# Pooled attention and an affine ResMLP on one core: loads moved to ScalarE's queue, and q's last rows transposed directly behind the fourth chunk of u

## Chip, cores and metric

The kernel runs on one NeuronCore of a Trainium2 chip. The metric is device time in microseconds: the median of seven runs is 348.65 us (345.37 to 350.87). The engines are named as in the profile: PE is TensorE, DVE VectorE, ACT ScalarE, POOL GpSimd, SP SyncE. SP computes nothing here, it issues DMAs; ACT and POOL can issue DMAs too. PEld is the loading of weights into PE.

## The reference: what is computed

Eight batches of attention with 8 heads, 576 rows and a head width of 64, whose keys and values are first averaged over groups of 8 rows (72 groups). Its result, with the heads side by side as 512 columns, goes through token mixing over the 576 rows and a two-layer network with 2048 hidden columns:

```
k_p = k.reshape(B, H, Sp, pool, D).mean(axis=3)        # pool = 8, Sp = 72
v_p = v.reshape(B, H, Sp, pool, D).mean(axis=3)
scores = scale * np.matmul(q, k_p.transpose(0, 1, 3, 2))
attn = softmax(scores);  x = attn @ v_p                # heads side by side: (B, 576, 512)
a1 = alpha1 * x + beta1
u = x + lam * np.einsum('ts,bsd->btd', w_tok, a1)
ch = np.maximum((alpha2 * u + beta2) @ w_ch1, 0.0) @ w_ch2
out = u + lam * ch
```

Inputs and output are float32; matrix products run in 16-bit types.

## The kernel before

**Chunks and blocks.** The output rows are cut into chunks of 128: four for each batch (rows 0 to 511), and one that holds the last 64 rows of two neighbouring batches (c = 4, made in the odd batch). The 36 chunks are lined up and taken four at a time, so there are nine blocks n = 0 to 8. A block runs the network on four chunks: `mlp_A(n, j)` (L640) makes hidden tile j of 16 (four matmuls into ps_h at L651, a relu to Hj on ACT at L657), and `mlp_B(n, m, part)` (L662) makes the output of chunk m in four parts of four matmuls (ps_ch, L686). After part 3, DVE adds the result to u (L692, L693) and SP stores it (L695, L699).

**Attention of the next batch inside the block.** Block n also works on batch b = n + 1, through `attention(b)` (L789): sums of v (DVE, L479) and of k (POOL, `sum_k`, L183 and L185), pooled keys (`att_K`), scores (`att_S4`, L500, which reads qT for the first 512 rows at L511 and rem_qT for the last 64 at L518), exponentials on ACT, the product with v (`att_AV`), x_tm on DVE (L563) and xs = x times lam and alpha1 (`att_X`, L577). Then `mix_T(b, c)` (L602) does token mixing: five matmuls into ps_tok that read xs (L609), then u_sb (L613) and u_bf (L616) on DVE. `mix_uT` (L618) transposes u_bf into u_fm, the input of a later block: from block 1 on as a crossbar (transposing) DMA on SP (L625). The chunks made in block n are used in block n + 1 in part: block 1 needs all four chunks of batch 1, block 2 the first three of batch 2 and the shared chunk before them, block 3 again the first three of batch 3, later blocks fewer of the newest batch.

**Loads.** In block n the inputs of batch b + 1 = n + 2 are loaded: q for rows 0 to 511 by POOL with a cast to bf16 (`load_q_bf`, L79), k by `load_k` (L88, two DMAs of 512 KB), v by `load_v` (L153), and the last 64 rows of q and k by `load_rem` (L141, four DMAs of 64 KB). Up to now k, v and the last rows go out on SP, except at the start. POOL's `cast_rem` (L164) turns the last rows into rem_q and rem_k; `att_Frem` (L410) transposes rem_q into rem_qT by a crossbar DMA on SP (L415) from b = 2 on; `att_F` (L382) does it for q's main part (L391).

**What sets the order.** The tile pools have a manual schedule: each piece of work carries a number, its place in the block, and L875 sorts the list and emits it. The sort is stable, and the items of mlp_A and mlp_B are put into the list first (L841 to L850), so at equal numbers they come first. mlp_A(j) has place j, mlp_B in blocks from 1 on 16 + 4m + part. In block 0 the first two chunks alternate:

```
        for m in range(4):
            for part in range(4):
                at = 16 + (2 * part + m if n == 0 and m < 2 else 4 * m + part)
                todo.append((at, lambda m=m, part=part: mlp_B(n, m, part)))
```

Each engine and each issuing queue then goes through its own instructions in that order. `first` in `attention` is b == 1, that is block 0. The places beside the change: mlp_B in block 0 at 16 to 31; the store of a chunk comes with its part 3; `mix_uT` has the place of its mix_T plus 1.8; `cast_rem(b + 1)` is at 24.5 (25.6 in block 0), `sum_k(b + 1)` at -0.9 and 0.3 of the next block, directly followed on POOL by that block's q loads at 0.4 and 0.5. On ACT the last work of a block from 1 on is at 15.35 (the last exponentials), the next is the first Hj of the next block.

Of the kernel before, what the change touches and what calls it, by code (L numbers as in the profile page):

```python
# [23 lines left out]
def kernel(  # L24
# [18 lines left out]
    nc = tc.nc  # L43
# [8 lines left out]
    def gp(name):  # L52
        return psA.tile([P, 512], FP, tag="gp", name=name)
# [17 lines left out]
    def rows(src, b, u):  # L71
        return src[b, 4 * u:4 * u + 4, 0:512, :].rearrange("h (p c) d -> p h (c d)", c=4)
# [15 lines left out]
    def load_k(b, u, behind=None, queue=nc.sync):  # L88

        raw = work.tile([P, 4, 4, D], FP, tag="k_raw", bufs=2, name="k_raw")  # L90
        if behind is not None:
            behind.memset(raw[:, 0, 0, 0:1], 0.0)
        queue.dma_start(out=raw.rearrange("p h c d -> p h (c d)"), in_=rows(k, b, u))
        st1[b]["raw"][u] = raw
# [46 lines left out]
    def load_rem(b, queue=nc.sync, behind=None):  # L141

        raw = work.tile([P, 2, 2, 2, D], FP, tag="rem_raw", bufs=2, name="rem_raw")
        if behind is not None:
            behind.memset(raw[:, :, :, 0, 0:1], 0.0)
        for i, src in enumerate((q, k)):
            for h in range(2):
                (nc.scalar if h and not b else queue).dma_start(
                    out=raw[:, i, h].rearrange("p c d -> p (c d)"),
                    in_=src[b, h::2, 512:576, :].rearrange("a (i c) d -> i a (c d)", c=2))  # L150
        st1[b]["rem_raw"] = raw
# [12 lines left out]
    def cast_rem(b, eng, copy=None):  # L164
        raw = st1[b]["rem_raw"]
        rq = work.tile([P, 2, 2, D], BF, tag="rem_q", bufs=2, name="rem_q")
        rk = work.tile([P, 2, 2 if b else 3, D], BF, tag="rem_k", bufs=2, name="rem_k")
        (copy or eng.tensor_copy)(out=rq.rearrange("p c h d -> p h c d"), in_=raw[:, 0])
        twice = [raw[:, 1, :, c].unsqueeze(2).to_broadcast((P, 2, 2, D)) for c in range(2)]
        if b:  # L170
            eng.tensor_tensor(out=rk, in0=twice[0], in1=twice[1], op=ALU.add)
        st1[b]["rem"] = rq, rk
# [190 lines left out]
    def load_w2(g):  # L363
        nc.gpsimd.dma_start(
            out=w2[g], in_=moe_w_ch2[512 * g:512 * g + 512, :].rearrange("(p i) d -> p i d", i=4))

    def scale_w2(g):
        nc.vector.tensor_tensor(
            out=w2[g], in0=w2[g], in1=lam_bc.unsqueeze(1).to_broadcast((P, 4, DM)), op=ALU.mult)
# [40 lines left out]
    def att_Frem(b, copy=None):  # L410

        st = st1[b]
        st["rem_qT"] = work.tile([P, 2, P], BF, tag="rem_qT", bufs=2, name="rem_qT")
        if copy is None:
            nc.sync.dma_start_transpose(out=st["rem_qT"],  # L415
                                        in_=st["rem"][0].rearrange("p c h d -> p (c h d)"))
            return
        ps_q = gp("ps_qr").bitcast(BF)
        for c in range(2):
            nc.tensor.transpose(out=ps_q[:, 128 * c:128 * c + 128],  # L420
                                in_=st["rem"][0][:, c].rearrange("p h d -> p (h d)"),
                                identity=identity_bf)
        copy(out=st["rem_qT"], in_=ps_q[:, 0:256].rearrange("p (c t) -> p c t", c=2))
# [365 lines left out]
    def attention(b):  # L789


        first = b == 1
        todo = []
        if first:
            for hp in range(4):
                todo.append((2.6 + 0.9 * hp, lambda hp=hp: att_F(b, hp)))
            todo.append((3.5, lambda: cast_rem(b, nc.gpsimd)))
            for u in range(2):
                todo.append((3.65 + 0.1 * u, lambda u=u: load_w2(2 + u)))
            todo.append((7.4, lambda: att_Frem(b, nc.scalar.copy)))  # L800
        if b < B - 1:
            at = 28.5 if first else 10.0
            todo.append((at, lambda: att_F(b + 1, 0)))
            todo.append((at + 0.1, lambda: att_F(b + 1, 2)))
            todo.append((25.6 if first else 24.5, lambda: cast_rem(b + 1, nc.gpsimd)))
            todo.append((27.5, lambda: att_Frem(b + 1)))
        for u in range(2):
            todo.append((3.6 + 0.1 * u if first else -0.9 + 1.2 * u,
                         lambda u=u: sum_k(b, u, nc.gpsimd)))
            todo.append((7.0 + 2.3 * u if first else 4.1 + 2.0 * u,  # L810
                         lambda u=u: att_K(b, u, nc.vector.tensor_copy)))
        for u in range(2):
            at = (9.0 if first else 6.3, 13.6)[u]
            todo.append((at, lambda u=u: att_S4(b, u)))
            for k, dt in enumerate((0.1, 0.1, 0.1, 0.7, 1.7, 1.75) if u else (0.1, 0.1, 0.1, 1.1, 2.1, 3.1)):
                todo.append((at + dt, lambda u=u, k=k: st1[b]["exp", u](k)))
            early = (5.7, 6.2, 4.2, 4.7) if first else (5.7, 6.2, 2.9, 3.4)
            for i, dt in enumerate((2.9, 3.4, 4.6, 5.1) if u else early):
                h = 4 * u + i
                todo.append((at + dt, lambda h=h: att_AV(b, h)))  # L820
                if i % 2:
                    eng = nc.gpsimd if h == 5 or first and h < 5 else nc.vector
                    todo.append((at + dt + 0.1, lambda h=h, eng=eng: att_X(b, h - 1, h + 1, eng)))
        if first:
            for i, u in enumerate((0, 2, 1)):
                todo.append((10.6 + 0.1 * i, lambda u=u: sum_v(b, u)))
            for u in range(2):
                todo.append((12.3 + 1.0 * u, lambda u=u: first_V(b, u)))
        for hp in range(0 if first else 4):
            todo.append((0.2 + 2.0 * hp, lambda hp=hp: att_V(b, hp)))  # L830
        for c in range(5):
            at = 21.0 + 1.3 * c
            if c < 4 or b % 2:
                todo.append((at, lambda c=c: mix_T(b, c)))
                key = (b, c) if c < 4 else (b - 1, 4)
                todo.append((at + 1.8, lambda key=key: mix_uT(key)))
        return todo

    for n in range(NBLK):
        todo = []  # L840
        for j in range(0 if n else 4, NJ):  # L841
            if n == 0 and j < 8:
                todo.append((j, lambda j=j: mlp_A(0, j, 0, 256)))
                todo.append((j + (1.01 if j < 7 else 0.3), lambda j=j: mlp_A(0, j, 256, 512)))
            else:
                todo.append((j, lambda j=j: mlp_A(n, j)))
# [4 lines that stand above are left out]
        if n == 0:  # L851
            todo.append((6.2, lambda: setup_rowsum(4)))
            todo.append((8.3, setup_wtok_odd))
            for g in range(2, 4):
                todo.append((4 * g - 0.8, lambda g=g: setup_bias(range(4 * g, 4 * g + 4))))
        if n == NBLK - 1:
            for g in range(4):
                todo.append((2.0 + 3.0 * g, lambda g=g: scale_w2(g)))
        b = n + 1
        if b < B:  # L860
            todo += attention(b)
            if b + 1 < B:
                new_batch(b + 1)
                gate = nc.vector if b == 1 else None
                for u in range(2):
                    at = (15.31 if b == 1 else 21.0) + 0.01 * u
                    todo.append((at, lambda b=b, u=u: load_k(b + 1, u, gate)))
                    at = {1: 14.0, 2: 6.5}.get(b, 0.4) + 0.1 * u
                    todo.append((at, lambda b=b, u=u: load_q_bf(
                        b + 1, u, nc.vector if b == 2 else None)))  # L870
                    at = 15.35 + 0.01 * u if b == 1 else (6.7 if b == 2 else 3.5) + 4.0 * u
                    todo.append((at, lambda b=b, u=u: load_v(
                        b + 1, u, behind=nc.vector if b < 3 else None)))
                todo.append((15.3 if b == 1 else 20.9, lambda b=b: load_rem(b + 1, behind=gate)))
        for _, do in sorted(todo, key=lambda x: x[0]):  # L875
            do()

# [29 lines left out]
```

## Time and profile before

| | us |
|---|---|
| median of seven runs | 348.65 |
| lowest, highest | 345.37, 350.87 |
| the profiled execution | 349.64 |
| its span | 347.9 |
| PE busy in it | 339.4 |
| DVE, ACT, POOL busy | 222.1, 146.7, 94.4 |

The profiled execution is about 1 us longer than the median. Its span leaves out 1.7 us around the program. TensorE was granted its full clock nearly throughout (mean 0.999). "Busy" counts instructions, not useful work, and the ends of matmuls are modelled: the next one starts before the end of the one before, so starts are the surer numbers. A DMA's line on SP, ACT or POOL is its issue; when the data arrive is seen in whoever waits for it. In the chain of waits, a line with "DMA" is the time from issue to landing.

Limits of the blocks in this execution (by the first matmul of mlp_A): block 0 from 31.7, block 1 from 71.7, block 2 from 106.9, block 3 from 143.55, block 4 from 178.9, block 5 from 215.35, block 6 from 252.36, block 7 from 288.86, block 8 from 316.49 to 344.2 us. An even batch's block takes about 35.2 us, an odd one's about 36.5, for it mixes a fifth chunk.

### The profile page before, as it was taken

What the parts mean: (1) busy time and instruction counts of PE and PEld (TensorE: products, weight loads), DVE (VectorE), ACT (ScalarE), POOL (GpSimd) and SP (SyncE); (2) the same over time, 40 slices, a digit from 0 to 9 for tenths busy, and PEclk for the clock granted to TensorE, in tenths of its full rate; (3) what the DMA queues carried; (4) which work ended last, traced back from release to release, by engine and by line L of the source; (5) the groups of instructions that cost most, each with busy time, mean ns of one, the idle gap of its engine ahead of it and who ended that gap; (6) DMA issues with size and microseconds to landing.
All of it is one profiled execution on the core that took longest, in us unless ns stands there. A gap on an engine that the chain in (4) does not pass through costs nothing.

```text
span 347.9 us, 5882 instructions
## 1 busy us (share of the span) xinstructions
PE 339.4 (98%) x2204; PEld 180.3 (52%) x2204; DVE 222.1 (64%) x477; ACT 146.7 (42%) x277; POOL 94.4 (27%) x110
## 2 busy tenths in 40 slices
PE   6999999999999999999999999899999999999995
PEld 2776854455445544455445544454455445545544
DVE  5575177986687668876867597658685882037511
ACT  2574980058304830385028501690079105704700
POOL 8477727601135011801170117001600100000000
PEclk9999999999999999999999999999999999999999
DMA  8999949967678914796489436981910032011012
GB/s 119 195 246 260 263 89 225 229 153 131 136 207 183 177 32 134 181 225 77 145 179 209 66 116 189 176 133 48 241 54 1 32 90 75 2 60 61 2 48 73
DMA packets 66030, 45.76 MB, mean 132 GB/s; under 512 B 34345, under 2 KB 56237, under 8 KB 66002
## 3 DMA queue, kind: packets, MB, share of 16 engines
q1 hardware_dynamic: 51716, 32.73, 39.2%
q0 software_dynamic: 13824, 12.40, 21.8%
q8 instruction: 17, 0.28, 0.3%
q10 hardware_dynamic: 462, 0.27, 0.3%
q14 instruction: 11, 0.09, 0.1%
HBM read 38.30 MB, written 9.44 MB: 137 GB/s over the span
## 4 chain that ended last, share of the span: by engine, by line
PE 91%; DMA 4%; DVE 3%; issue 1%; POOL 0%; SPq 0%; POOLq 0%
PE ps_h L651 35%; PE ps_ch L686 33%; PE ps_tok L609 11%; PE ps_av L555 2%; PE ps_s L511 2%; DMA rem_qT<-rem_q 2%; DMA q_bf<-in_q_dram 2%; PE ps_ch L675 1%; PE ps_sc L491 1%; PE ps_kp L439 1%; PE ps_q L396 1%; DVE u_sb L613 1%; PE ps_r L518 1%; DVE u_bf L616 1%; PE ps_av L559 1%; PE ps_v L466 1%
## 5 line engine op out<-in xcount | busy, mean ns | idle before, releaser
L657 ACT ACTIVATE Hj<-ps_h,bias_cols 128x512 bf16<-128x512 f32 x144 | 98.2, 688 | 165.1 <-PE ps_h L651 163.5
L651 PE MATMUL ps_h<-u_fm,w 128*128 128x512 bf16 (+2 forms) x608 | 133.6, 368 | 0.4 <-DVE bias_cols L654 0.2
L686 PE MATMUL ps_ch<-w,Hj 128*128 128x512 bf16 x560 | 130.9, 379 | 0.0
L651 PEld LDWEIGHTS <-w 128*128 128x128 bf16 x608 | 65.6, 114 | 51.4 <-issue 3.3
L686 PEld LDWEIGHTS <-Hj 128*128 128x128 bf16 x560 | 52.9, 98 | 61.6 <-issue 1.6
L609 PE MATMUL ps_tok<-xs,wtT 128*128 128x512 bf16 (+3 forms) x200 | 44.9, 380 | 0.1
L577 POOL TENSOR_TENSOR xs<-x_tm,lamal_bc 128x512 bf16<-128x512 f32 x12 | 15.2, 1268 | 109.0 <-DVE x_tm L563 108.8
L692 DVE TENSOR_TENSOR ps_ch<-lam_bc,ps_ch 128x512 f32<-128x512 f32 x32 | 22.1, 692 | 33.4 <-PE ps_ch L686 33.2
L561 DVE RECIPROCAL rec<-ps_av 128x5 f32<-128x5 f32 x64 | 12.2, 191 | 35.0 <-PE ps_av L559 34.6
L613 DVE TENSOR_TENSOR u_sb<-x_tm,ps_tok 128x512 f32<-128x512 f32 (+1 forms) x40 | 27.3, 683 | 10.8 <-PE ps_tok L609 10.6
L563 DVE TENSOR_TENSOR x_tm<-ps_av,rec 128x320 f32<-128x320 f32 x64 | 31.5, 491 | 2.7
L693 DVE TENSOR_TENSOR u_sb<-u_sb,ps_ch 128x512 f32<-128x512 f32 x35 | 24.0, 687 | 13.6 <-PE ps_ch L686 12.5
L540 ACT ACTIVATE ET<-ps_s 72x512 f16<-72x512 f32 x56 | 32.3, 591 | 0.0
L609 PEld LDWEIGHTS <-wtT 128*128 128x128 bf16 (+3 forms) x200 | 17.3, 100 | 21.2 <-issue 1.7
L616 DVE TENSOR_TENSOR u_bf<-u_sb,al_bc 128x512 bf16<-128x512 f32 x34 | 26.5, 778 | 2.5 <-DMA u_fm<-u_bf 1.4
L479 DVE TENSOR_TENSOR v_u<-v_u 72x512 f32<-72x512 f32 (+1 forms) x48 | 26.4, 550 | 0.8
L183 POOL TENSOR_TENSOR k_raw<-k_raw 128x512 f32<-128x512 f32 x14 | 18.5, 1324 | 9.5 <-DMA k_raw<-in_k_dram 9.5
L555 PEld LDWEIGHTS <-ET 72*128 72x128 f16 x256 | 14.5, 100 | 9.2 <-DVE x_tm L563 0.5
L185 POOL TENSOR_TENSOR k_bf<-k_raw 128x512 bf16<-128x512 f32 x14 | 18.8, 1341 | 1.1
L79 POOL DMA_DIRECT2D q_bf<-in_q_dram x16 | 12.5, 783 | 15.1 <-DVE v_u L158 13.6
L555 PE MATMUL ps_av<-vp,ET 72*128 72x66 f16 x256 | 16.1, 196 | 0.0
L577 DVE TENSOR_TENSOR xs<-x_tm,lamal_bc 128x512 bf16<-128x512 f32 x20 | 14.7, 737 | 0.7
(130 smaller groups left out, 221.0 us busy)
## 6 DMA issues: line engine op xcount, KB each, us to landing
out_dram<-u_sb SPq DMA_DIRECT2D x32, 256.0 KB
k_raw<-in_k_dram SPq DMA_DIRECT2D x12, 512.0 KB
v_u<-in_v_dram SPq DMA_DIRECT2D x12, 512.0 KB
q_bf<-in_q_dram POOLq DMA_DIRECT2D x16, 256.0 KB, 6.3
w<-in_moe_w_ch_dram POOLq DMA_DIRECT2D x6, 512.0 KB, 8.8
w<-in_moe_w_ch_dram POOLq DMA_DIRECT2D x1, 1024.0 KB, 14.1
k_raw<-in_k_dram POOLq DMA_DIRECT2D x2, 512.0 KB, 14.0
v_main<-in_v_dram POOLq DMA_DIRECT2D x1, 1024.0 KB, 7.8
```

The source lines that it names most:

```text
L479: nc.vector.tensor_tensor(out=t[:, :, 0:n], in0=t[:, :, 0:n], in1=t[:, :, n:2 * n], op=ALU.add)
L540: nc.scalar.activation(out=o, in_=i, func=AF.Exp, bias=0.0, scale=0.125)
L555: nc.tensor.matmul(out=av[:, odd + c, :], lhsT=ET[:, m0:m0 + 128], rhs=vp1[:, hh, :])
L563: nc.vector.tensor_tensor(out=x[:, 1 - odd:6 - odd, dd:dd + D], in0=av[:, :, 0:64], in1=rec.unsqueeze(2).to_broadcast((P, 5, D)), op=ALU.mult)
L577: eng.tensor_tensor(out=xs[:, 0:4, cols], in0=x[:, 1:5, cols], in1=lamal_bc[:, cols].unsqueeze(1).to_broadcast((P, 4, D * (h1 - h0))), op= ...
L609: nc.tensor.matmul(out=ps_tok[p0:p1], lhsT=wtT[0:kk, at, P * c:P * c + p1 - p0], rhs=xs_pool[i][0:kk, sc, :], start=(sc == 0), stop=(sc == 4))
L613: nc.vector.tensor_tensor(out=s["u"][p0:p1, :], in0=x[p0:p1, 1 + c if c < 4 else 5 - 5 * i, :], in1=ps_tok[p0:p1, 0:DM], op=ALU.add)
L616: eng.tensor_tensor(out=s["u_bf"], in0=s["u"], in1=al2_bc, op=ALU.mult)
L651: nc.tensor.matmul(out=ps_h[:, t0:t1 + one], lhsT=w1_of(cc, j), rhs=rhs, start=(cc == 0), stop=(cc == 3))
L657: nc.scalar.activation(out=t, in_=ps_h, func=AF.Relu, bias=bias_cols[:, j:j + 1], scale=1.0)
L686: nc.tensor.matmul(out=ps, lhsT=Hj[n, j][:, 128 * m:128 * m + 128], rhs=w2[j // 4][:, j % 4, :], start=(j == 0), stop=(j == NJ - 1))
L693: nc.vector.tensor_tensor(out=u, in0=u, in1=ps, op=ALU.add)
```

## The change

Four edits in the lists of work. In block 0 the numbers of `mix_T` go from 21.0 + 1.3c to 20.8 + 1.2c, and those of `mix_uT` with them. `att_Frem(b + 1)` goes from 27.5 to 26.72 (26.22 in block 0), where it follows the `mix_uT` of c = 3. The loads of k and of the last rows for batches 3 to 7 are issued by ACT in place of SP, and their numbers go from 21.0 and 20.9 to 20.1 and 20.0. Batch 2's loads, made in block 0, stay on SP.

```
@@ -803,7 +803,7 @@
             todo.append((at, lambda: att_F(b + 1, 0)))
             todo.append((at + 0.1, lambda: att_F(b + 1, 2)))
             todo.append((25.6 if first else 24.5, lambda: cast_rem(b + 1, nc.gpsimd)))
-            todo.append((27.5, lambda: att_Frem(b + 1)))
+            todo.append((26.72 if b > 1 else 26.22, lambda: att_Frem(b + 1)))
         for u in range(2):
             todo.append((3.6 + 0.1 * u if first else -0.9 + 1.2 * u,
                          lambda u=u: sum_k(b, u, nc.gpsimd)))
@@ -829,7 +829,7 @@
         for hp in range(0 if first else 4):
             todo.append((0.2 + 2.0 * hp, lambda hp=hp: att_V(b, hp)))
         for c in range(5):
-            at = 21.0 + 1.3 * c
+            at = 20.8 + 1.2 * c if first else 21.0 + 1.3 * c
             if c < 4 or b % 2:
                 todo.append((at, lambda c=c: mix_T(b, c)))
                 key = (b, c) if c < 4 else (b - 1, 4)
@@ -863,15 +863,17 @@
                 new_batch(b + 1)
                 gate = nc.vector if b == 1 else None
                 for u in range(2):
-                    at = (15.31 if b == 1 else 21.0) + 0.01 * u
-                    todo.append((at, lambda b=b, u=u: load_k(b + 1, u, gate)))
+                    at = (15.31 if b == 1 else 20.1) + 0.01 * u
+                    todo.append((at, lambda b=b, u=u: load_k(
+                        b + 1, u, gate, nc.sync if b == 1 else nc.scalar)))
                     at = {1: 14.0, 2: 6.5}.get(b, 0.4) + 0.1 * u
                     todo.append((at, lambda b=b, u=u: load_q_bf(
                         b + 1, u, nc.vector if b == 2 else None)))
                     at = 15.35 + 0.01 * u if b == 1 else (6.7 if b == 2 else 3.5) + 4.0 * u
                     todo.append((at, lambda b=b, u=u: load_v(
                         b + 1, u, behind=nc.vector if b < 3 else None)))
-                todo.append((15.3 if b == 1 else 20.9, lambda b=b: load_rem(b + 1, behind=gate)))
+                todo.append((15.3 if b == 1 else 20.0, lambda b=b: load_rem(
+                    b + 1, nc.sync if b == 1 else nc.scalar, gate)))
         for _, do in sorted(todo, key=lambda x: x[0]):
             do()
 
```

More of the change, by code (lines that the diff above doesn't have):

```diff
@@ L805, in attention @@
             todo.append((25.6 if first else 24.5, lambda: cast_rem(b + 1, nc.gpsimd)))
-            todo.append((27.5, lambda: att_Frem(b + 1)))
+            todo.append((26.72 if b > 1 else 26.22, lambda: att_Frem(b + 1)))
         for u in range(2):
@@ L831, in attention @@
         for c in range(5):
-            at = 21.0 + 1.3 * c
+            at = 20.8 + 1.2 * c if first else 21.0 + 1.3 * c
             if c < 4 or b % 2:
@@ L865 @@
                 for u in range(2):
-                    at = (15.31 if b == 1 else 21.0) + 0.01 * u
-                    todo.append((at, lambda b=b, u=u: load_k(b + 1, u, gate)))
+                    at = (15.31 if b == 1 else 20.1) + 0.01 * u
+                    todo.append((at, lambda b=b, u=u: load_k(
+                        b + 1, u, gate, nc.sync if b == 1 else nc.scalar)))
                     at = {1: 14.0, 2: 6.5}.get(b, 0.4) + 0.1 * u
@@ L873 @@
                         b + 1, u, behind=nc.vector if b < 3 else None)))
-                todo.append((15.3 if b == 1 else 20.9, lambda b=b: load_rem(b + 1, behind=gate)))
+                todo.append((15.3 if b == 1 else 20.0, lambda b=b: load_rem(
+                    b + 1, nc.sync if b == 1 else nc.scalar, gate)))
         for _, do in sorted(todo, key=lambda x: x[0]):
```

## The prediction

> **What bounds the kernel now.** I read the page's busy shares first, then busy time by stage, then TensorE's waits, then the chain of waits through the one long wait, and last the queues around it. Busy time of each engine, from the page:
>
> ```profile
> PE 339.4 (98%) x2204; PEld 180.3 (52%) x2204; DVE 222.1 (64%) x477; ACT 146.7 (42%) x277; POOL 94.4 (27%) x110
> ```
>
> TensorE is busy 339.4 of 347.9 us. The first 7.6 us (until q's first rows land) and the last 3.7 us (output stores) are outside the change. Cut into blocks n (one pass over 16 hidden tiles and the next batch's attention), with length, then PE's busy time (instructions):
>
> ```profile
> 178.90:215.35 36.45, 36.45 (x236) 18.47 (x234) 27.88 (x55) 15.09 (x28) 10.66 (x12) 1.00 0.63 136
> 215.35:252.36 37.01, 35.44 (x226) 18.09 (x225) 24.70 (x52) 15.09 (x28) 8.54 (x10) 1.00 0.81 149
> 252.36:288.86 36.50, 36.50 (x235) 18.52 (x234) 27.10 (x55) 15.12 (x28) 2.25 (x3) 1.00 0.15 41
> ```
>
> Only block n=5 (from 215.35) has a hole: 37.01 - 35.44 = 1.57 us. PE's own waits name it:
>
> ```profile
> PE ps_r L518 <- DMA rem_qT<-rem_q: 1.6, 1, 1.6
> PE ps_q L396 <- DMA q_bf<-in_q_dram: 1.3, 1, 1.3
> ```
>
> The second is the start. The first is one of six crossbar transfers of q's last rows. The chain of waits through it (start, length, what):
>
> ```profile
> 212.47 1.41 DVE u_bf L616
> 213.91 0.71 DVE ps_ch L692
> 214.64 0.70 DVE u_sb L693
> 215.36 0.38 SPq L695
> 215.84 7.70 DMA rem_qT<-rem_q
> 223.58 0.26 PE ps_r L518 x2
> ```
>
> The transfer sits on SyncE behind an output store (L695) that waits for VectorE's last step on that chunk. It starts at 215.84, flies 7.70 us, and PE had reached its reader at about 222.0. SyncE's queue ahead of it, and what GpSimd issues then:
>
> ```profile
> 202.80 1.22 SPq L148 DMA_DIRECT2D rem_raw<-in_q_dram  x2
> 204.07 1.25 SPq L148 DMA_DIRECT2D rem_raw<-in_k_dram  x2
> 205.41 1.09 SPq L93 DMA_DIRECT2D k_raw<-in_k_dram  x2
> 206.59 1.22 SPq L625 DMA_TRANSPOSE u_fm<-u_bf  x1
> 209.14 3.95 SPq L625 DMA_TRANSPOSE u_fm<-u_bf  x3
> 214.96 1.55 POOL L79 DMA_DIRECT2D q_bf<-in_q_dram  x2
> ```
>
> So the late transfer also flies beside 512 KB of q. The other five are not waited for. Two smaller holes: 0.15 us at 143.40 (chain, "issue", before the first ps_h of block 3), and in block 0, on PE and VectorE:
>
> ```profile
> 54.44 2.75 PE L686 MATMUL ps_ch<-w,Hj 128*128 128x512 bf16 x12
> 57.26 1.25 PE L609 MATMUL ps_tok<-xs,wtT 128*128 128x512 bf16 x5
> ```
> ```profile
> 55.87 1.33 DVE L577 TENSOR_TENSOR xs<-x_tm,lamal_bc 128x512 bf16<-128x512 f32 x1
> ```
>
> At 0.216 us a matmul (four take 0.86 in the chain) the twelve are issued through 54.44 + 12 x 0.216 = 57.03; ps_tok starts at 57.26, just after xs ends at 57.20. It is at the edge: already 0.23 us late.
>
> **What the Trainium skill says.** (1) "DMA: Bandwidth & Descriptors", Queues, rings and completion order: SP and ACT each own a row of rings; within a ring descriptors are taken in order, and a DMA engine takes turns between rows, packet by packet. The trace agrees with the first half: issued at 136.49 behind 1 MB of k, u's first transpose in block 2 lets VectorE's u_bf go (L616, waiting for "DMA u_fm<-u_bf") only at 141.79, 5.3 us later. (2) Same page, Issuing engines are not separate DMA queues: another issuing engine saves only issue time, the 16 DMA engines are shared. So no bandwidth is gained; only order and hour change. (3) "Perfetto Trace Analysis", DMA Instruction — HWDGE: the profiled span is the issue, not the movement. It agrees: 1.21 us issue against 7.70 us to landing. (4) "TensorE: Matmul & The Clock Gate", What overlaps and what doesn't: matmuls keep strict order. No trace line here goes against it, and it makes the block-0 edit below costly.
>
> **Part 1: loads from ScalarE (b = 2 to 6, five blocks).** Removed from SyncE in each block: four last-row issues and two k issues, 1.22 + 1.25 + 1.09 = 3.6 us. Added to ScalarE: six issues; ACT's own last-row issues at the start took 0.616 and 0.680 us, so 4 x 0.65 + 1.09 = 3.7 us. What is queued behind them is block n+1's first Hj, 19.07 us later (ACT idle 197.24 to 216.31), so they cost ScalarE nothing. Without that cover they would cost 3.7 us a block. Their buffers were freed in the block before (sum_k of b ended by 179.5), so nothing waits.
>
> The hour matters more. SyncE reached the loads only after the store at 202.37, which waits for a sum; ScalarE reaches them at 197.24, 5.6 us earlier, when the DMA rate is 0 GB/s (197 to 201). With the flights of now (last q rows 3.1 us from first issue to GpSimd's cast, k 4.0 us): rem_q cast at 200.4, k sums 203.9 to about 209.1, and GpSimd's next q load, queued behind the sums, at 209.2 instead of 214.96. SyncE's transposes then run when VectorE frees them: u's third at 209.5, fourth at 210.8.
>
> **Part 2: rem_qT directly behind the fourth u transpose.** It passes one output store; the store (and in odd batches u's fifth transpose) goes 1.2 us later at most, read a block or more later: nothing. With part 1 rem_qT issues at 210.8 + 1.27 = 212.1, not 215.84. At the same 7.7 us it lands at 219.8, before 222.0, with 2.2 us to spare. **Gain: -1.57 us.** Its q rows are cast at 200.4, long ready. What is late next in these blocks: u's transpose that opens the next block. Block 2 is tightest: the third one (issued about 139.7 now, needed at 143.4) goes at 136.75. The 0.15 hole closes: **-0.15 us**. But the q load moves into that stretch (137.2 instead of 145.35); a flight over 6.65 us would wait. Flights seen: 3.9 here at most, 5.3 behind k, 7.7 beside q. Bounds: 0 to +1.05 us; I take 0, because by 137.2 the transpose is already issued.
>
> **Part 3: block 0 (b = 1).** mix_T moves from 21.0 + 1.3c to 20.8 + 1.2c. The list sorts stably: at 21.0 mlp_B(0, 1, 2) came first, at 20.8 it comes behind. So ps_tok is reached one part (4 matmuls, 0.86 us) earlier, at 54.44 + 8 x 0.216 = 56.17, while xs still ends at 57.20 (x_tm follows attention matmuls that don't move). PE waits 1.09 us instead of 0.23: **+0.86 us**, and everything behind keeps its order with PE full until the block ends. Chunks 1 to 3 keep their PE places; the fifth comes one part earlier, harmless. The cover that it gives up was that part. In return: rem_qT(2) no longer waits for the store at 70.92 (it goes about 2.4 us earlier), qT(2) about 0.4 us earlier, and the reader comes 0.86 later. None of them was waited for: 0 in this trace; in another execution up to some 1 us, since u's fourth transpose landed only about when the queue ran empty at 70.5, needed at 71.5.
>
> **Sum.** -1.57 - 0.15 + 0.86 = -0.86 us. The profiled execution took 349.64 us for a span of 347.9 (1.7 around it), 1 us above the median of 348.65. I apply the difference to the median: 348.65 - 0.86 = 347.8 us.
>
> **Rivals.**
> - A (0.55), as above: 347.8; own range 346.8 to 348.8.
> - B (0.22): late transfers cost more in unprofiled executions than in this one. For: the runs spread from 345.37 to 350.87, 5.5 us, more than the 1.9 us of holes outside the start. Then the move gains as much as lies from the median to the fastest runs (345.4): about 3.3 us, and a little more if the block-0 wait is partly made up: 345.0. Against: part of the spread can be the start (6.27 us for q's first rows).
> - C (0.11), the other side: q's load, now beside u's transposes, makes the block's opening transposes late. Price if each flies 7.7 us: block 2 +1.05, block 1 (issued at 101.5, needed at 106.74) +2.5, with block 0's 0.86 less 1.57: +2.8, so 351.5. It decides when flights pass 6.65 us in block 2 and 5.2 in block 1. Against: in block 1 q's load comes only at about 104, behind late k.
> - D (0.12): the median run has no 1.57 hole; only block 0's wait remains: 348.65 + 0.86 = 349.5.
>
> **How the numbers follow.** One per cent (3.5 us) is about what a measurement of this kernel can tell from no change. A and D are within it; of B I put 0.18 below 345.2; of C half above 352.1, with 0.02 for an unknown stall in each of the five blocks. Faster 0.19, same 0.73, slower 0.08. The range takes in A, D, most of B and the low end of C: 345.0 to 350.0.
>
> **What would show it.** Right: k and last-row issues on ACT's queue at about 197 in block 4 (5 to 6 us before the old hour); rem_qT right behind u's fourth transpose and no wait of L518; no wait of u_bf for u_fm; q_bf issued near 209; PE waiting about 1.1 us for xs at 56 with ps_ch x8 ahead of it. Wrong: ps_tok in block 0 starts on time; PE waits for u_fm at 107 or 143; or the hole at 222 stays.

## The result and the profile after

The changed kernel was slower, not a little faster. Beside each other on one chip the medians are 349.62 us (345.33 to 354.04, 27 executions) after the change and 347.1 us (343.05 to 352.21, 64 executions) before it; the ratio is 1.008 with a 95% interval of 1.0059 to 1.010. The forecast was 347.8 us, 0.86 us below the 348.65 us of the first seven executions. The profiled execution took 348.38 us for a span of 346.4 us.

A ratio here leaves out executions that lie more than 1.5% above the fastest of their kernel; since the loss found below comes in some executions and not in others, the tables give over all executions the difference of the means to the kernel before on the same chip, with its 95% interval, and the share above 349 us (single executions of 493, 888 and 1963 us are left out).

Busy time of each engine, from the page after:

```profile
PE 337.3 (97%) x2204; PEld 178.2 (51%) x2204; DVE 227.6 (66%) x477; ACT 146.8 (42%) x277; POOL 98.1 (28%) x110
```

VectorE has the same 477 instructions and is busy 5.5 us longer, GpSimd has the same 110 and is busy 3.7 us longer: no work was added, so something slows both. TensorE's own waits (line, what it waited for: us in total, times, longest):

```profile
PE ps_h L651 <- DMA u_fm<-u_bf: 1.4, 1, 1.4
...
PE ps_tok L609 <- DVE xs L577: 0.9, 1, 0.9
```

The 1.6 us for rem_qT at L518 are gone. Two waits have come: one for u's transposes at the opening of a block, one for xs in block 0. (At the start a wait of 0.6 us for wt_bf has come too, and the one for q's first rows fell from 1.3 to 0.6 us; the change does not touch either.) Busy time by stage, blocks 3 and 4, with length, then busy time of PE, PEld, DVE, ACT and POOL (instructions), granted clock, DMA share and GB/s:

```profile
142.32:178.93 36.61, 35.21 (x225) 17.89 (x223) 27.85 (x54) 15.09 (x28) 10.48 (x10) 1.00 0.75 139
178.93:215.61 36.68, 36.68 (x235) 18.59 (x236) 26.61 (x54) 15.09 (x28) 10.51 (x10) 1.00 0.73 147
```

Block 3 now has the hole, 36.61 - 35.21 = 1.40 us, at its very end, where block 4 is to open; before, it took 35.35 us. Block 5, where the old hole was, has no wait in the list any more. The chain of waits through the new hole (start, length, what):

```profile
170.18 0.69 DVE ps_ch L692
...
170.90 0.70 DVE u_sb L693
...
171.61 0.37 SPq L695
...
172.03 6.85 DMA u_fm<-u_bf
...
178.93 4.51 PE ps_h L651 x20
```

It has the same shape as the chain that held rem_qT: VectorE's last step on a chunk, its store on SyncE, and behind the store a crossbar transfer that flies long, here 6.85 us. But now the transfer is u's, and a whole block opens with it: block 4 begins with chunks 0 and 1 of batch 4 among its four (L56 to L60), so of the three transposes that go out together it needs the first. (Block 3 needs the first two.) What else is on the queues then, on ScalarE (the loads), GpSimd, SyncE and VectorE, each from its own timeline:

```profile
158.87 0.55 ACTq L148 DMA_DIRECT2D rem_raw<-in_q_dram  x1
...
161.50 1.08 ACTq L93 DMA_DIRECT2D k_raw<-in_k_dram  x2
```
```profile
167.99 1.72 POOL L183 TENSOR_TENSOR k_raw<-k_raw 128x512 f32<-128x512 f32 x1
169.79 1.60 POOL L185 TENSOR_TENSOR k_bf<-k_raw 128x512 bf16<-128x512 f32 x1
171.33 1.55 POOL L79 DMA_DIRECT2D q_bf<-in_q_dram  x2
```
```profile
172.03 4.49 SPq L625 DMA_TRANSPOSE u_fm<-u_bf  x3
176.62 1.20 SPq L415 DMA_TRANSPOSE rem_qT<-rem_q  x1
```
```profile
166.99 1.59 DVE L616 TENSOR_TENSOR u_bf<-u_sb,al_bc 128x512 bf16<-128x512 f32 x1
```

k goes out at 161.50, where SyncE had reached it at 169.92. So GpSimd's sums of k end by 171.33 instead of 179.4, and the q load queued behind them, 512 KB, starts at 171.33 instead of 179.38: it now leaves 0.70 us ahead of the three transposes, the first of which block 4 waits for. And while the sums run, VectorE's u_bf, 0.69 us in all four chunks of this block before, takes up to 1.59 us, and GpSimd's sums up to 1.72 us where they took 1.26 to 1.41.

Block 0, on TensorE and VectorE:

```profile
52.51 1.89 PE L686 MATMUL ps_ch<-w,Hj 128*128 128x512 bf16 x8
55.33 1.25 PE L609 MATMUL ps_tok<-xs,wtT 128*128 128x512 bf16 x5 [0.93 <-DVE xs L577]
```
```profile
53.94 1.33 DVE L577 TENSOR_TENSOR xs<-x_tm,lamal_bc 128x512 bf16<-128x512 f32 x1
```

Eight ps_ch lie ahead of the first ps_tok instead of twelve, xs ends at 55.27, and TensorE waits 0.93 us.

### The profile page after: what moved, and what is told of

The parts are those of the page before. It is cut to its first block, busy times and chain, and to the rows that moved or that the text cites. A ratio compares the mean times of both kernels' runs of the same rounds, so it can differ in the third digit from the quotient of the medians.

```text
span 346.4 us, 5889 instructions
## 1 busy us (share of the span) xinstructions
PE 337.3 (97%) x2204; PEld 178.2 (51%) x2204; DVE 227.6 (66%) x477; ACT 146.8 (42%) x277; POOL 98.1 (28%) x110
## 4 chain that ended last, share of the span: by engine, by line
PE 89%; DMA 5%; POOL 2%; DVE 2%; issue 1%; SPq 0%; POOLq 0%
PE ps_h L651 36%; PE ps_ch L686 33%; PE ps_tok L609 10%; DMA wt_bf<-in_moe_w_tok_dram 3%; PE ps_s L511 2%; PE ps_av L555 2%; DMA u_fm<-u_bf 2%; PE ps_ch L675 1%; PE ps_r L518 1%; PE ps_w L325 1%; DVE u_sb L613 1%; PE ps_av L559 1%; PE ps_kp L439 1%; POOL v L113 0%; POOL k L85 0%
## 5 line engine op out<-in xcount | busy, mean ns | idle before, releaser
L692 DVE TENSOR_TENSOR ps_ch<-lam_bc,ps_ch 128x512 f32<-128x512 f32 x32 | 22.1, 691 | 32.3 <-PE ps_ch L686 32.1
L693 DVE TENSOR_TENSOR u_sb<-u_sb,ps_ch 128x512 f32<-128x512 f32 x35 | 24.0, 686 | 13.6 <-PE ps_ch L686 12.5
L613 DVE TENSOR_TENSOR u_sb<-x_tm,ps_tok 128x512 f32<-128x512 f32 (+1 forms) x40 | 27.3, 682 | 8.4 <-PE ps_tok L609 8.3
L616 DVE TENSOR_TENSOR u_bf<-u_sb,al_bc 128x512 bf16<-128x512 f32 x34 | 30.0, 882 | 1.2
L183 POOL TENSOR_TENSOR k_raw<-k_raw 128x512 f32<-128x512 f32 x14 | 20.5, 1465 | 8.3 <-DMA k_raw<-in_k_dram 8.3
L79 POOL DMA_DIRECT2D q_bf<-in_q_dram x16 | 12.6, 790 | 15.7 <-DVE v_u L158 14.9
```

The costliest lines, as they stand in the source:

```text
L613: nc.vector.tensor_tensor(out=s["u"][p0:p1, :], in0=x[p0:p1, 1 + c if c < 4 else 5 - 5 * i, :], in1=ps_tok[p0:p1, 0:DM], op=ALU.add)
L616: eng.tensor_tensor(out=s["u_bf"], in0=s["u"], in1=al2_bc, op=ALU.mult)
L693: nc.vector.tensor_tensor(out=u, in0=u, in1=ps, op=ALU.add)
```

## The experiments

"Before" in a diff is the kernel before unless another is named. The loads in the first tests are those of part 1; q's load is GpSimd's, at L79.

**The two halves and the single parts.** First the block-0 edit alone:

```
-            todo.append((27.5, lambda: att_Frem(b + 1)))
+            todo.append((27.5 if b > 1 else 26.22, lambda: att_Frem(b + 1)))
-            at = 21.0 + 1.3 * c
+            at = 20.8 + 1.2 * c if first else 21.0 + 1.3 * c
```

> Only the block-0 edits: mix_T at 20.8 + 1.2c and q's last rows of batch 2 right behind u's fourth transpose; all loads stay on SyncE. Theory T1 (block 0 gives up one mlp_B part as cover for xs, the earlier loads cost the rest): PE waits about 0.9 us for xs at about 56 us, and the time is 0.86 us above before, a ratio of about 1.0025. Rival R1 (the whole loss comes from block 0): ratio 1.007 to 1.008. Rival R2 (the loss comes from moving rem_qT ahead of the store in all blocks): about 1.0025 or less here.

Then the change without it (mix_T back at 21.0 + 1.3c, att_Frem at 26.72 in every block):

> The change without its mix_T edit in block 0 (mix_T back at 21.0 + 1.3c, rem_qT at 26.72 in every block). T1: no wait for xs; what is left of the loss comes from q's loads beside u's transposes and from GpSimd's sums beside VectorE's u_bf: ratio about 1.005, and PE waits for u_fm at the opening of a block in some executions. R1: ratio 1.000 or below (0.997 if the hole of rem_qT is gone too). R2: like T1 in time, but rem_qT late, not u_fm.

Then part 1 alone, the loads from ScalarE with att_Frem left at 27.5:

> Only the loads of k and of the last rows from ScalarE; mix_T and rem_qT at their old places. T1: ratio 1.004 to 1.006, with q's loads near 208 us in block 4 and u_bf slower on VectorE. R1: 1.000 or below. R2: 1.000 or below, since the store stays ahead of rem_qT.

And part 2 alone, one number changed in the kernel before:

```
-            todo.append((27.5, lambda: att_Frem(b + 1)))
+            todo.append((26.72, lambda: att_Frem(b + 1)))
```

> Only rem_qT directly behind u's fourth transpose, in every block; mix_T and loads as before. T1: 0 to 1.6 us less, ratio 0.996 to 1.000, no wait of PE for rem_qT. R1: the same. R2: slower, 1.004 to 1.008, with stores or u's fifth transpose late behind it.

| kernel | executions | median us | mean less before, us | above 349 us | ratio (95%) |
|---|---|---|---|---|---|
| the change | 27 | 349.62 | +2.17 ± 0.85 | 18 of 27 | 1.008 (1.0059 to 1.010) |
| block-0 edit alone | 22 | 347.93 | +0.65 ± 0.81 | 5 of 22 | 1.003 (1.0001 to 1.006) |
| change without block 0 | 22 | 347.52 | +0.68 ± 1.31 | 8 of 22 | 0.9979 (0.9946 to 1.0013) |
| loads alone (part 1) | 22 | 347.99 | +0.98 ± 1.13 | 9 of 22 | 1.0012 (0.9979 to 1.0044) |
| rem_qT alone (part 2) | 14 | 346.39 | -0.93 ± 0.85 | 0 of 14 | 0.9989 (0.9957 to 1.002) |

Part 2 gains, and the loads take more than that back: that is what the column of means says, though in it no interval but the change's own and part 2's is clear of zero. The ratios fit the expectations only in part. The block-0 edit's 1.003 does, and it speaks against the rival that puts the whole loss there, which asked for 1.007 to 1.008. But 0.9979 and 1.0012 for the two kernels with the loads lie below the 1.004 to 1.006 that were expected of them. The profiles say what happens. In the block-0 kernel the wait for rem_qT is still there, 1.3 us, so the old hole is no accident of one profile; in the kernel with the loads alone it is gone, without part 2. And that kernel's profile has the new hole at its worst. Its chain of waits, then its busy time in two stretches (length, busy PE, PEld, DVE, ACT, POOL, granted clock, DMA share, GB/s):

```profile
170.72 8.31 DMA u_fm<-u_bf
179.07 7.46 PE ps_h L651 x20
```
```profile
179.00:186.00 7.00, 6.93 (x19) 2.59 (x20) 1.29 (x3) 2.29 (x4) 0.00 (x0) 0.56 0.70 184
186.00:190.00 4.00, 4.00 (x39) 2.44 (x38) 3.09 (x7) 3.22 (x7) 0.00 (x0) 1.00 0.00 0
```

The transposes fly 8.31 us, TensorE waits 3.0 us, and the next twenty matmuls take 7.46 us at a granted clock of 0.56, where the same twenty took 4.51 us behind the shorter hole of the change. The wait costs 3.0 us and the clock after it about another 3.0 us. The Trainium skill has this, "TensorE: Matmul & The Clock Gate", Part 1: The HAM clock gate (the "warmup" mystery): after an idle window, for which it gives some 3.4 us, TensorE runs at half speed until it has been busy for a window. This run agrees in kind; here 3.0 us of idling were enough.

**Is it q's load?** The new theory was that the q load, pulled forward by the sums of k, delays the transposes; the rival was that the slow u_bf does it, since it issues the transposes later. A second rival was that k's packets, now from ScalarE's queue, take turns with the transposes. Three kernels part them, each built on the change without block 0. In the first, q's load is held back by a VectorE instruction that writes one element of its target (the gate that batch 3's load has already); nothing else is edited:

```
-                        b + 1, u, nc.vector if b == 2 else None)))
+                        b + 1, u, nc.vector if b > 1 else None)))
```

> Loads from ScalarE and rem_qT as in the change, mix_T of block 0 as before, and the q loads of blocks 2 to 4 held back by a VectorE memset at place 0.4 of their block, about where they were issued before (some 145 us in block 2). Theory T2 (q's load flying beside u's transposes makes the transposes late): no wait of PE for u_fm at the opening of blocks 3, 4 and 5, no executions above about 349 us, median 345.5 to 346.5, ratio 0.995. Rival R3 (GpSimd's earlier sums slow VectorE's u_bf, so that the transposes are issued late): waits for u_fm stay at about half their size or more, and so does a median of 347.5. Rival R4 (k on ScalarE's ring takes turns with SyncE's transposes): all stays, since k's hour is not changed.

In the second, q's load goes ahead of the sums; in its profile it leaves 6.9 us ahead of the transposes in blocks 2 and 3, but only 2.4 us in block 1:

```
-                    at = {1: 14.0, 2: 6.5}.get(b, 0.4) + 0.1 * u
+                    at = {1: 14.0, 2: 6.5}.get(b, -1.0) + 0.01 * u
```

> The same without the memset, but the q loads of batches 4 and later stand ahead of the k sums on GpSimd (place -1.0), so they are issued right after the cast of the last rows, near 201 us in block 4 in place of 208. T2: q has landed before u's second transpose; no wait for u_fm in blocks 3 to 5; median 345.5 to 346.5, ratio 0.995. R3: the sums go 1.5 us later only, VectorE's u_bf stays slowed, the waits for u_fm stay at half or more. R4: worse or the same as the change without its block-0 edit, for more lands at the hour of k.

In the third, the sums are also held until VectorE is through with u_bf (a gate at place 26.9: VectorE writes one element of k_bf in each partition, and GpSimd writes it again before the sum). Of the edit only the call is shown:

```
+            if not first:
+                todo.append((26.9, lambda: hold_sums(b + 1)))
```

> As the one with q early, and GpSimd's k sums are held back (a VectorE memset at place 26.9, and a small GpSimd memset) until VectorE has made the last u_bf of the block. T2: the same time as with q early, within 0.2 per cent. R3: u_bf at 0.69 us each again, u's transposes 1 to 2 us earlier in blocks 3 and 4, and 1 us or more faster than with q early.

With them ran the change itself once more:

> The changed kernel as it is, beside these three on one chip. Both T2 and R3: ratio about 1.005 to 1.008; against the version without the block-0 edit (0.998 by the fast runs, half of them above 348) it should show 0.9 us for block 0 and no more. If it comes out at 1.003 or less, the rest of the first measurement was chance in how many executions had late transposes.

| kernel | executions | median us | mean less before, us | above 349 us | ratio (95%) |
|---|---|---|---|---|---|
| q late | 22 | 345.29 | -1.65 ± 0.99 | 2 of 22 | 0.9948 (0.992 to 0.9976) |
| q early | 22 | 345.62 | -1.51 ± 0.76 | 0 of 22 | 0.9967 (0.9942 to 0.9993) |
| q early, sums late | 22 | 346.2 | -1.44 ± 0.81 | 1 of 22 | 0.9961 (0.9936 to 0.9987) |
| the change again | 14 | 348.66 | +1.79 ± 1.82 | 7 of 14 | 1.0005 (0.9964 to 1.0047) |

Moving q's load away from the transposes, to either side, turns the loss into a gain. Moving the sums as well adds nothing that these intervals show, although it does what it should: every u_bf takes 0.69 us again, and in block 3 TensorE is ready for the transposes 6.55 us after their start instead of 5.68. The kernel with q late keeps the slow u_bf, so the slow u_bf alone costs nothing that shows. It keeps k's hour and queue as well, so k's packets alone are not the cause either.

**The same collision without the loads, the remedy in the full change, and the last cell.** q's load beside the transposes in the kernel before, with no load moved to ScalarE (the edit of "q early", in the kernel before, where k comes late):

> The kernel before, with one edit: q's loads of batches 4 and later stand ahead of the k sums on GpSimd (place -1.0), with k and the last rows still on SyncE. They are issued near 208 us in block 4, the same hour as in the change, beside u's transposes; the sums stay as late as before (209 us on). T2 (q's load beside u's transposes suffices): a mean 1.5 us or more above before, a third or more of the executions above 349 us, PE waits for u_fm of 1.5 us or more at the opening of blocks 2 to 5 in some. R3 (it takes the earlier sums): no slower than before, within 0.5 us.

The full change, block 0 included, with q late:

> The change as it is, with block 0's edits, and the q loads held back by VectorE at place 0.4 as in the run with q late. T2 and block 0: 0.9 us above the version with q late and mix_T of block 0 at its old place (which runs beside it), so a ratio of 0.997 to 0.998 against before, and one wait of 0.9 us for xs in the profile. If it is at 1.005 or above, the q load was not the cause.

"Q late" once more:

> The version with q late again (mix_T of block 0 as before), as the other side of the pair: ratio 0.9948 as in its first measurement, within 0.2 per cent, and hardly an execution with a mean TensorE clock below 0.996.

And q's load beside the transposes with the sums held back, so that u_bf is fast (the third kernel above, with the loads of batch b + 2 at place 22.9 of block b behind a VectorE gate):

```
+                    if 1 < b < B - 2:
+                        todo.append((22.9 + 0.01 * u, lambda b=b, u=u: load_q_bf(
+                            b + 2, u, nc.vector)))
```

> As the one with q early and the sums late, but the q loads of batches 4 to 7 are put at place 22.9 of the block before and held by a VectorE memset behind u's second u_bf, near 169 us in block 3: beside u's transposes, while no k sum slows VectorE. T2: waits for u_fm come back, mean 1 us or more above the one with q early and sums late. R3: as fast as that one (mean 346.0). If it takes both, a late issue and a long flight, it lies between, with holes under 1.5 us and no clock lost.

| kernel | executions | median us | mean less before, us | above 349 us | ratio (95%) |
|---|---|---|---|---|---|
| before, q beside u | 6 | 358.82 | +12.5 ± 2.0 | 6 of 6 | 1.0337 (1.0275 to 1.0399) |
| change, q late | 22 | 344.86 | -1.17 ± 0.89 | 1 of 22 | 0.9978 (0.9951 to 1.0006) |
| q late again | 22 | 345.02 | -1.75 ± 0.89 | 1 of 22 | 0.9954 (0.9927 to 0.9981) |
| q beside u, sums late | 21 | 346.75 | -0.02 ± 0.85 | 2 of 21 | 0.9998 (0.9971 to 1.0025) |

The first row shows the collision without a load on ScalarE. TensorE's waits and one step of its chain:

```profile
PE ps_h L651 <- DMA u_fm<-u_bf: 9.9, 4, 3.7
```
```profile
144.53 6.88 DMA u_fm<-u_bf
```

Four blocks open late, 9.9 us in all. In this kernel k's sums come after q's load, and of the u_bf ahead of the transposes the first two take 0.69 us and the third 0.84 us at most, so neither ScalarE's loads nor slow u_bf is needed for the loss. (It isn't a clean copy of the change's collision: k's late loads fly in the same stretch.) And q late, block 3 into 4, on GpSimd, SyncE and in the chain of waits:

```profile
179.28 1.55 POOL L79 DMA_DIRECT2D q_bf<-in_q_dram  x2 [8.49 <-DVE q_bf L78]
```
```profile
170.09 4.70 SPq L625 DMA_TRANSPOSE u_fm<-u_bf  x3
```
```profile
176.05 4.32 PE ps_h L651 x20
```

The transposes go out at 170.09, and TensorE opens block 4 at 176.05 straight out of its matmuls: the first of them needed at most 5.96 us, against 6.85 us in the change and 8.31 us in the loads alone. The first profile of q late has the sharper case, on VectorE, SyncE and TensorE:

```profile
170.81 1.52 DVE L616 TENSOR_TENSOR u_bf<-u_sb,al_bc 128x512 bf16<-128x512 f32 x1
```
```profile
175.78 4.37 SPq L625 DMA_TRANSPOSE u_fm<-u_bf  x3
```
```profile
181.18 4.48 PE L651 MATMUL ps_h<-u_fm,w 128*128 128x512 bf16 x19
```

Here u_bf is slow and the transposes are as late as in the change: TensorE is ready 5.40 us after their start, where in the change it was ready after 5.50 us (178.93 - 1.40 - 172.03). Yet no hole follows; the transpose landed in time. What differs in these queues is q's load, which leaves at 184.57. (This execution took 350.48 us, but the 5.3 us by which its span is longer than the other's lie ahead of 84 us.)

In the last row of the table, q beside u with fast u_bf, the loss is not there but neither is the gain. In its profile q leaves 1.48 and 1.49 us ahead of the transposes in blocks 3 and 2, and no hole follows. Its one hole for u_fm, 1.24 us at the opening of block 2, is no sign of q's new hour: "q early, sums late" has one of 1.16 us in the same place, with q issued 5.9 us ahead, and what makes these two is not shown. From that kernel, which differs in little but q's hour, it lies some 1.4 us away in the mean (-0.02 ± 0.85 against -1.44 ± 0.81, on another chip). Set against the change without block 0, a little less than 1 us could be the sums' part, within the intervals.

**The sizes again.** The halves' intervals were as wide as what they were to tell, so four kernels ran again on one chip: the change, its two halves, and part 2 alone.

> The changed kernel, beside its two halves on one chip. If block 0 (0.9 us) and the collision of q with u's transposes (about 1 us in the mean) simply add: a mean 1.5 to 2.5 us above before, a half of the executions above 349 us. If the parts work on one another: 1 us or more above the sum of the two halves.

> The change without its mix_T edit. Adding: a mean 0.5 to 1.5 us above before, a third of the executions above 349 us. If the loss is block 0's alone: at or below before, under a quarter above 349 us.

> Only block 0's edits. Adding: 0.5 to 1.0 us above before (the wait of 0.9 us less what rem_qT of batch 2 may gain). If block 0's edit costs more than its wait, through later blocks: 1.5 us or more.

> Only rem_qT directly behind u's fourth transpose. As in its first measurement 0.5 to 1.5 us below before in the mean, and hardly an execution above 349 us; if that was chance, the same as before.

| kernel | executions | median us | mean less before, us | above 349 us | ratio (95%) | mean less before, all measurements |
|---|---|---|---|---|---|---|
| the change | 22 | 348.68 | +1.56 ± 1.04 | 10 of 22 | 1.0011 (0.9977 to 1.0045) | +1.91 ± 0.62 |
| change without block 0 | 22 | 348.28 | +1.12 ± 1.26 | 8 of 22 | 0.9988 (0.9956 to 1.002) | +0.91 ± 0.91 |
| block-0 edit alone | 20 | 347.77 | +0.77 ± 0.81 | 3 of 20 | 1.0015 (0.9989 to 1.0042) | +0.71 ± 0.57 |
| rem_qT alone | 22 | 345.48 | -1.22 ± 0.77 | 1 of 22 | 0.9957 (0.9931 to 0.9982) | -1.09 ± 0.57 |

The last column pools the two or three measurements of a kernel; q late pools to -1.71 ± 0.66. The halves add up: +0.71 + 0.91 = +1.62 against +1.91. Over part 2 alone the loads cost +0.91 - (-1.09) = +2.0 us in the mean, and with q late that is gone: between the change without block 0 and q late lie 2.6 ± 1.1 us. The ratios, which leave out the long executions, point the same way with less room: 0.9948 and 0.9954 for q late against 0.9979 and 0.9988. The change's own ratio of 1.008 did not come again; it was 1.0005 and 1.0011, so its loss rests on the means and on how many executions are long.

**Why in some executions only.** Six profiles have ScalarE's loads and q's old place in GpSimd's queue. Read from SyncE's and GpSimd's timelines, this is the start of the three transposes and of q's load in blocks 2 and 3, at whose ends the holes of the change lie, and the hole behind it on TensorE:

| profile | block 2: u, q | hole | block 3: u, q | hole |
|---|---|---|---|---|
| the change | 134.35, 134.98 | none | 172.03, 171.33 | 1.40 |
| the change again | 134.06, 134.68 | none | 170.86, 171.50 | none |
| the change, third | 133.05, 132.33 | 1.59 | 171.49, 170.79 | 1.58 |
| without block 0 | 131.44, 132.05 | none | 168.23, 168.88 | none |
| without block 0, second | 133.99, 134.61 | none | 170.84, 171.49 | none |
| loads alone | 133.28, 133.91 | none | 170.72, 170.02 | 3.00 |

Where the transposes leave 0.61 to 0.65 us ahead of q there is no hole, eight times of eight; where q leaves 0.70 to 0.72 us ahead of them there is one of 1.4 to 3.0 us, four of four. Without block 0, GpSimd and SyncE of block 3:

```profile
168.88 1.55 POOL L79 DMA_DIRECT2D q_bf<-in_q_dram  x2
```
```profile
168.23 3.90 SPq L625 DMA_TRANSPOSE u_fm<-u_bf  x3
```

The order of the two lines is the reverse of the change's above, and the three transposes are issued in 3.90 us instead of 4.49. The lead differs too: in block 3 TensorE was ready 5.35 to 5.50 us after the transposes' start where there is a hole, 6.17 to 6.23 us where there is none. That is a part of the hole only: TensorE opened 6.9 to 8.35 us after the start in these three, which would have left holes of 0.7 us or more even with the longer lead. Nor is the order the whole rule. In block 4 q leaves 0.17 us ahead in five of the six profiles and 1.52 us in the third of the change; there TensorE is ready only 6.0 to 7.1 us after the start, and only the loads alone have a hole, of 0.33 us. (In the third profile of the change the trace puts both waits down to VectorE's L693, which ended just before. That is not what TensorE needs: in the first profile L693 ran from 178.37 to 179.06, and ps_h had started at 178.93.)

What tips it seems to be the contest between VectorE and GpSimd. In the four cases with a hole one of the first two u_bf took 1.59 to 1.80 us; in the eight without, 1.29 us at most. The Trainium skill, "GPSIMD Engine Reference", 1. Specifications, says that GpSimd shares its SBUF interfaces with VectorE and contends with VectorE's instructions of two SBUF inputs. The trace agrees: u_bf reads two such inputs and slows down, while L613, L692 and L693, with an input from PSUM, keep 0.67 to 0.70 us in the same stretch. That this contest decides the order is read from these twelve cases and not shown; no run changed it alone.

## Why the prediction was wrong

**The step that failed** is the end of part 2, where the new hour of q's load was priced: "Block 2 is tightest ... Bounds: 0 to +1.05 us; I take 0, because by 137.2 the transpose is already issued." Nothing was wrong with the hours: q was forecast for 209.2 in block 4 and came at 208.31. Wrong was to price one block and to put the term at 0; in its place the loads with q's new hour measured +2.0 ± 1.1 us over part 2 alone. Block 3 was not worked out at all, and there the load comes at 171.33 beside transposes at 172.03. Its margin could be had from the trace of before: the transpose that block 4 needs, the first of three, went at 173.00 for a need at 178.75, so a flight above 5.75 us would show, less than block 2's 6.65. A store stood ahead of these three, and still does, so earlier loads could win little there: in the change the margin was 5.50 us. Nor did the reason given hold in block 2 itself: in the third profile of the change q left 0.72 us ahead of the three transposes there, and the hole was 1.59 us. The text even had the warning in block 4, q at 209.2 and u's third transpose at 209.5, and did not read it as a toss-up. The expected place of a load was treated as an order.

**Part 1** (0, bounds 0 to +1.05 us) was right about its own costs: ScalarE issues the six loads from 158.87 on and nothing behind them is late, and the old hole closes by the loads alone. With the effect on q's load it cost the 2.0 ± 1.1 us, at or above its upper bound. Two things were not in that bound: the sums of k now run beside u_bf, and in one profile a hole of 3.0 us was followed by a granted clock of 0.56, which cost about another 3.0 us.

**Part 2** (-1.57 - 0.15 us) was right in mechanism: rem_qT is issued right behind the fourth u at 212.55 (forecast 212.1) and nobody waits for it. Alone it measured -1.09 ± 0.57 us. With the loads and q late, parts 1 and 2 together measured -1.71 ± 0.66 us, against -1.72 forecast; with such an interval, and q at an hour that the forecast did not have, the agreement in the second digit is luck.

**Part 3** (+0.86 us) was right: TensorE waits 0.93 us (forecast 1.09) for xs behind ps_ch x8, and the edit alone measured +0.71 ± 0.57 us.

So the sum of -0.86 us agrees with what is measured once the collision is taken away: the change with q late came to -1.17 ± 0.89 us. That the 349.62 us of the change lie within the stated 345.0 to 350.0 us is no merit of the sum, which pointed the other way.

**The rivals.** C, at 0.11, named the mechanism, "q's load, now beside u's transposes, makes the block's opening transposes late", but in blocks 1 and 2, always, and at 351.5 us. It came at the ends of blocks 2 and 3 (the openings of 3 and 4), in some executions. D, that the median execution has no hole at L518, is not supported: the wait of 1.3 to 1.7 us is in all three profiles that keep the loads on SyncE and the old places of rem_qT and q (before, block 0 twice). B's 345.0 us is about what q late reaches, 345.0 to 345.3, but by parts 1 and 2 as priced, on chips where the kernel before also ran below the 348.65 us shown; late transfers that cost 3.3 us were not seen in any kernel that keeps q's old hour.

**What stays open.** Why q's packets delay transposes that are issued 0.7 us behind them, and not those issued 0.65 us ahead or (with fast u_bf) 1.48 us behind, is not shown by any run. How much of the loss belongs to the slow u_bf is bounded only: nothing that shows with q late, some 1 us or nothing beside q. The change's own size varies between its measurements (means +2.17, +1.79 and +1.56 us), as it would if it depends on a toss-up, though their intervals overlap. Where the last kernel with q beside u loses its gain, and why two kernels open block 2 late by 1.2 us, is not shown.

## What to carry to other kernels

When a load is issued earlier, follow what its consumer releases: here k's load freed GpSimd's sums, these freed the next load in GpSimd's queue, and that one met the transfers that open a block; its new hour has to be held against the need of every block, not of one. Where two chains come out within a microsecond of each other, as q's load and u's transposes do, price both orders and give the order itself by a wait, as the gate on q's load does: it was one line, and the kernel without the block-0 edit then ran at 0.9948 and 0.9954 of the time before. A hole on TensorE is not priced by its length alone: holes up to 1.6 us cost their length here, those of 3.0 us and more were followed by slow matmuls.

## What the hardware showed that was not expected

- Holes of 1.2 to 1.6 us left the clock alone (the twenty matmuls behind took 4.48 to 4.51 us); holes of 3.0, 3.36 and 3.69 us were followed by twenty matmuls in 7.46, 6.12 and 7.30 us. These three come from two profiles, of executions of 351.88 us (the loads alone) and 361.99 us (before, q beside u); the granted clock in the 6.1 to 7.3 us behind each was 0.56, 0.73 and 0.61.
- Beside GpSimd's sums of k VectorE's u_bf went from 0.69 to as much as 1.80 us, and beside GpSimd's work on the last rows (L168, L171) a 64x128 product of two SBUF tiles (L570) from 0.29 to 1.17 us; GpSimd's sums of k went from 1.27 to as much as 1.81 us. The two engines lose time together that the count of instructions does not show.
- ScalarE's queue issues its loads while its own last exponentials still run: the first load goes at 158.87, and two exponentials start at 159.57.
